# Two-layer cached attention and token mixer on one core: the last query tile of seven weights as two 64-row tiles, loaded in slices of 8 rows

## The chip, the core and the metric

The kernel runs on one core of a Trainium2 chip. A core has a matrix engine (TensorE, PE in the profile, with its weight loads PEld), a vector engine (VectorE, DVE), a scalar engine (ScalarE, ACT), GpSimd (POOL) and SyncE (SP), which here does nothing but issue transfers. Sixteen DMA engines move data between HBM and the on-chip memory (SBUF, 128 partitions). The metric is the device time of one execution in microseconds (us).

## The reference

Four blocks in a row on a state of 2 x 1 x 512 numbers: attention over a cache, mixer, attention, mixer. Both attention blocks read the same caches and the same weights.

```python
def _A_ref(x, k_cache, v_cache, wq, wo):          # B=2, D=512, 32 query heads, 8 KV heads
    q = (x @ wq).reshape(B, Sq, Hq, Dh)            # Dh=128, four query heads per KV head
    scores = q . k_cache * Dh ** -0.5              # 32768 cached keys per head
    o = softmax(scores) . v_cache
    return o.reshape(B, Sq, Hq * Dh) @ wo

def _B_ref(x, w1, b1, w2, b2):                     # mixer over a token axis of length 1, F=1792
    u = gelu(einsum("bsd,sf->bdf", layernorm(x), w1) + b1)
    return (einsum("bdf,fs->bds", u, w2) + b2).transpose

x = x + _A_ref(layernorm(x), ...)
x = x + _B_ref(layernorm(x), ...)
x = x + _A_ref(layernorm(x), ...)
x = x + _B_ref(layernorm(x), ...)
```

All numbers are float32. K and V together are 537 MB and are read in both layers; with the weights 1,067 MB go over the DMA engines (a few chunks stay on chip from one layer to the next).

## The kernel before

**Units and chunks.** A unit is one (layer, batch, KV head): 32 of them, in the order of the list `units`. The heads are split into `passing` (0, 1, 2, 3, 4, 6), whose units come first in layer 0 and last in layer 1, and `RESIDENT` (5, 7), whose units stand around the change of layer. A unit has 8 chunks of K and 8 of V, of 4,096 keys each; a chunk is 2 MB, 16 KB in each partition. `k_chunk` makes 8 products with a chunk of K, `v_chunk` 8 with one of V (16 rows each in the profile).

**Memory.** One tile `mem` holds 13 cells of 16 KB per partition and a rest of 5 x 2 KB. Cells 0 to 8 are the ring for K and V; cells 9 to 12 (`WCELL0`, `WCELLS`) hold the weights of up to four heads. In the middle of the run some cells and the rest keep a part of the K and V of head 7 (`KEPT_K`, `KEPT`).

**Weights.** For each head `wqo` has a row of 16 KB per partition: four tiles of wq (128 rows of the 512 inputs each, 512 columns) and four of wo. `load_weights` brings them in one transfer of 128 rows to one cell. `make_q` multiplies the normalised state `xnT` (128 partitions, 4 columns per batch) with the four wq tiles, each product a partial sum over 128 inputs; for passing heads both batches at once, the second one's query is kept (`q_kept`). `out_2` and `last_mixer` use the wo tiles through `wo_at`.

**The state.** `first_input` normalises the given state, which lies in 4 columns per batch. `to_columns` turns the row made by the mixer into such columns and normalises them into `xnT`.

**Order.** The kernel writes its own schedule. `stream` is the list of K and V loads in order; before the change of layer and after it a load is 4 chunks (8 MB) into one of two places of the ring, around the change it is one or two chunks. All work besides the chunks is entered by `at(time, f, ...)`, where time counts chunks; after each chunk `run(time)` emits what is due. A load of weights is entered 10 chunks before its unit's first K chunk (`kbeg[n] - 10`), the query's products 6 to 4 chunks before.

**SyncE's queue.** SyncE issues the loads in the order in which the program emits them. A K or V load waits until TensorE has finished with the chunks that lay in its place. Landings of loads are counted on eight semaphores in turn, so an issue also waits until the load eight issues earlier has landed. ScalarE issues three small transfers of its own: the state, the mixer's weights (`cols`) and one row of the output.

Of the kernel before, what the change touches and what calls it, by code (L numbers as in the profile page):

```python
# [13 lines left out]
P = 128  # L14
# [21 lines left out]
DIRECT = 2  # L36
TAIL_GROUPS = (3, 3, 3, 2, 1)
IDLE = (4, 1, 3, 2)
EPS = 1e-5


@with_exitstack
def gqa_mixer_kernel(ctx: ExitStack, tc: tile.TileContext, x, kt, v, wqo, cols, out):
# [38 lines left out]


    NP = 28 + 32 * 2
    widths = dict(x=B * DT, xn=B * DT, q=KEPT_Q * R, cols=4 * FT + 1, ident=P, one=1, half=1, selg=R * QT)
# [18 lines left out]
    def cells(k, m=1):  # L104
        return mem[:, k * CK : (k + m) * CK]

    def wq_at(h):
        return cells(home[h])[:, :W].rearrange("p (t c) -> p t c", t=DT)

    def wo_at(h):  # L110
        return cells(home[h])[:, W:].rearrange("p (t c) -> p t c", t=R)

    def load_weights(h, cell):
        home[h] = cell
        nc.sync.dma_start(cells(cell), wqo[h])


    used = [0] * (WCELL0 + WCELLS + 1)
# [80 lines left out]
    def first_input():  # L199

        t = spot()
        cen, sq = (t[:, k * B * DT : (k + 1) * B * DT].rearrange("p (b d) -> p b d", b=B) for k in range(2))
        m, rs = (t[:, (2 * DT + k) * B : (2 * DT + k + 1) * B] for k in range(2))
        p = misc()
        nc.tensor.matmul(p[:, : B * DT], ones, xcols.rearrange("p b d -> p (b d)"), start=True, stop=True)
        nc.vector.tensor_reduce(m, p[:, : B * DT].rearrange("p (b d) -> p b d", b=B), axis=AX.X, op=ALU.add)
# [4 lines left out]
        p = misc()  # L211
        nc.tensor.matmul(p[:, : B * DT], ones, sq.rearrange("p b d -> p (b d)"), start=True, stop=True)
        nc.vector.tensor_reduce(rs, p[:, : B * DT].rearrange("p (b d) -> p b d", b=B), axis=AX.X, op=ALU.add)
        nc.vector.tensor_scalar(rs, rs, 1.0 / D, EPS, op0=ALU.mult, op1=ALU.add)
        nc.gpsimd.tensor_tensor(rs, rs, half_neg.to_broadcast([P, B]), op=ALU.pow)
        for b in range(B):
            xT[b] = xcols[:, b, :]
            nc.vector.tensor_scalar_mul(xnT[:, :, b], cen[:, b, :], rs[:, b : b + 1])  # L218

    *ends, keeper = RESIDENT  # L220
# [30 lines left out]
    def to_columns(key):  # L251

        layer, b = key
        pt = misc()
        for d in range(DT):
            nc.tensor.matmul(  # L256
                pt[:, d : d + 1], ysb[key][:, d * P : (d + 1) * P], ident[:, :1], start=True, stop=True
            )
        nc.vector.tensor_scalar_add(xT[b], pt[:, :DT], b2c)
        mv, rs = stats[key]  # L260
        nc.vector.tensor_scalar(  # L261
            xnT[:, :, b], pt[:, :DT], mv[:, 0:1], rs, op0=ALU.subtract, op1=ALU.mult
        )

    def unit_of(n):

# [10 lines left out]
    def make_q(n, step, place=None):  # L277


        layer, b, h = unit_of(n)  # L280
        both = partner(n)
        m = 1 if both is None else B
        if n in q_kept:
            if step == 2:
                nc.vector.tensor_copy(qpad[n % 2][:, 28 : 28 + R], q_kept.pop(n))
            return
        if step == 0:

            q_ps[n] = pfix.tile([P, 512], F32, name="bcast") if N1 < n <= N3 + 2 else kept[0]
        if step < 2:  # L290
            for d in range(step * DT // 2, (step + 1) * DT // 2):
                nc.tensor.matmul(  # L292
                    q_ps[n][:m, :],
                    xnT[:, d, b : b + m],
                    wq_at(h)[:, d, :],
                    start=(d == 0),
                    stop=(d == DT - 1),
                )
# [234 lines left out]
    def out_2(n):  # L533
        layer, b, h = unit_of(n)
        for r in range(R):
            add_row(r, b, oT[n][:, r, :], wo_at(h)[:, r, :])

    ysb, px = {}, {}
    slope, shift, stats = {}, {}, {}
# [81 lines left out]
    def last_mixer(n):  # L621
# [9 lines left out]
        for k, to in enumerate((kept[1], acc)):  # L631
            for r in range(R):
                nc.tensor.matmul(
                    to[32 * r : 32 * r + 1, :w],
                    oT[n][:, r, 1:],
                    wo_at(h)[:, r, k * w : (k + 1) * w],
                    start=True,
                    stop=True,
                    skip_group_check=True,
                )  # L640
# [81 lines left out]
    def mix_4(key):  # L722

        layer, b = key
        p = px[key]
        nc.tensor.matmul(p, sel[b], ysb[key], start=False, stop=True, skip_group_check=True)
        if layer == LAYERS - 1:
            y = mem[:1, (WCELL0 + WCELLS) * CK :][:, :D]
# [166 lines left out]
def _layout(A_x, A_k_cache, A_v_cache, A_wq, A_wo, B_w1, B_b1, B_w2, B_b2):  # L895

    import numpy as np

    B, HKV, SK, DH = A_k_cache.shape
    D = A_x.shape[-1]  # L900
    n = SK // CK


    keys = np.arange(SK).reshape(n, CK)
    for c0, m in GROUPS:
        keys[c0 : c0 + m] = keys[c0 : c0 + m].reshape(P, m, CK // P).transpose(1, 0, 2).reshape(m, CK)
# [11 lines left out]
    return {  # L918
        "x": np.ascontiguousarray(A_x.reshape(B * (D // P), P).T),
        "kt": kt,  # L920
        "v": A_v_cache.reshape(B * HKV, SK * DH),
        "wqo": np.concatenate([wq.reshape(HKV, P, -1), wo.reshape(HKV, DH, -1)], axis=2),
        "cols": np.concatenate(cols, axis=1),
    }

# [24 lines left out]
```

## Time and profile before

| | |
|---|---|
| median of 3 runs | 2501.68 us (2501.5 to 2501.75) |
| the profiled execution | 2501.79 us |
| its span, first to last instruction | 2500.0 us |
| bytes moved by DMA | 1067.23 MB, mean 427 GB/s |
| TensorE busy | 1383.1 us (55%) |
| TensorE clock granted, mean | 0.773 |
| loads of weights | 14, of 2,048 KB, 33.8 us from issue to landing (median) |

How to read the profile. Its first part has the busy time of each engine and its share of the span. The second cuts the span into 40 slices; a digit is the busy share in tenths. The third has the DMA queues: q1 holds the transfers that SyncE issues, q10 those of ScalarE, q8 and q14 fetch instructions; the columns are packets, MB, and the time that the packets took as a share of 16 engines over the span. The DMA view can be cut to a stretch of the run: its packet counts and shares are then those of the packets that start in the stretch, and a share is of 16 engines over the stretch's length. A packet of 4 B is the mark by which one engine reports that its part of a transfer has landed. The fourth part follows back the chain of work that ended last. The rest are groups of instructions: line, engine, operation, names of output and inputs, shape, count, then busy time in us, mean duration in ns of one, and idle time of the engine before them. A float32 product appears as two rows of half the work. The timeline has start and duration in us. The windows view has, for each stretch, its length, the busy time and instructions of each engine (PE, PEld, DVE, ACT, POOL), the clock granted to TensorE, the mean busy share of the DMA engines and GB/s. The view of waits has, for an engine and a line, what it waited for, total us, times and the longest.

### The profile page before, as it was taken

The page shows a single profiled execution, that of the slowest core. Times are in us where ns is not written, and L with a number is a line of the kernel's source. Part 1 is how long each engine was busy: PE and PEld are TensorE (multiplying, and loading weights), DVE is VectorE, ACT ScalarE, POOL GpSimd, SP SyncE. Part 2 cuts the span into 40 slices and gives each one's busy share as a digit, 9 for nine tenths or more (in the row PEclk, how much of TensorE's full clock was granted, in tenths as well). Part 3 has the DMA queues.
Part 4 walks back from the last instruction along what each step waited for, and adds up shares of the span by engine and source line. Part 5 has one row for each costly group of instructions (what it writes and reads, how often), then busy time and mean ns, then how long its engine had stood idle before and what let it go on. Part 6 is the DMA issues. An engine that isn't in the chain of part 4 may idle for free.

```text
span 2500.0 us, 20528 instructions
## 1 busy us (share of the span) xinstructions
PE 1383.1 (55%) x9326; PEld 375.5 (15%) x9326; DVE 222.4 (9%) x610; ACT 185.4 (7%) x550; POOL 4.9 (0%) x17
## 2 busy tenths in 40 slices
PE   4545554645445554657667775455546454455546
PEld 1111111111111111111111211111111111111112
DVE  0000000000000000001111110000000000010002
ACT  0000000000000000001012010000000000011002
POOL 0000000000000000000000000000000000000000
PEclk8777777877777777879888977677778777777778
DMA  9999999999999999999999999999999999999996
GB/s 419 436 433 430 433 435 430 436 430 430 433 433 431 434 429 435 425 423 421 426 427 427 423 430 430 432 435 434 432 430 435 435 423 435 433 433 426 432 429 292
DMA packets 31200, 1067.23 MB, mean 427 GB/s; under 512 B 3717, under 2 KB 3721, under 8 KB 4618
## 3 DMA queue, kind: packets, MB, share of 16 engines
q1 hardware_dynamic: 30824, 1065.89, 99.2%
q8 instruction: 73, 1.20, 0.2%
q14 instruction: 13, 0.11, 0.0%
q10 hardware_dynamic: 290, 0.04, 0.0%
HBM read 1065.91 MB, written 0.00 MB: 426 GB/s over the span
## 4 chain that ended last, share of the span: by engine, by line
DMA 74%; PE 24%; issue 0%; DVE 0%; ACT 0%; SPq 0%; POOL 0%; ACTq 0%
DMA mem<-in_v_dram 65%; PE acc L492 19%; DMA mem<-in_kt_dram 9%; PE scores L359 3%; PE bcast L292 1%; PE rows L190 0%; PE small L385 0%; PE small L521 0%; ACT S L714 0%; PE kept L671 0%; PE small L379 0%; PE small L256 0%; ACT mem L681 0%; ACT mem L693 0%; PE bcast L575 0%
## 5 line engine op out<-in xcount | busy, mean ns | idle before, releaser
L359 PE MATMUL scores<-mem,small_sb 128*32 128x512 f32 x4096 | 620.6, 722 | 592.0 <-DMA mem<-in_kt_dram 591.6
L492 PE MATMUL acc<-mem,S 128*16 128x512 f32 x4088 | 614.1, 738 | 468.2 <-DMA mem<-in_v_dram 462.5
L359 PEld LDWEIGHTS scores<-mem,small_sb 128*32 128x32 f32 x4096 | 151.1, 127 | 970.5 <-issue 895.5
L396 ACT ACTIVATE S<-S,small_sb 128x128 f32<-128x128 f32 x240 | 123.5, 519 | 2102.4 <-DVE small_sb L387 1636.6
L492 PEld LDWEIGHTS acc<-mem,S 128*16 128x16 f32 x4088 | 134.8, 110 | 831.7 <-issue 693.2
L369 DVE TENSOR_REDUCE small_sb<-scores 128x1 f32<-128x512 f32 x64 | 44.2, 691 | 874.1 <-PE scores L359 874.1
L391 DVE STREAM_TRANSPOSE S<-scores 128x512 f32<-128x512 f32 x64 | 45.4, 710 | 131.4 <-PE acc L492 131.4
L292 PE MATMUL kept<-mem,small_sb 128*2 128x512 f32 x104 | 50.9, 615 | 1.7 <-DVE small_sb L218 1.7
L190 PE MATMUL rows<-mem,small_sb 128*1 128x512 f32 (+1 forms) x276 | 48.4, 603 | 3.1 <-ACT mem L714 2.4
L396 ACT ACTIVATION_READ_ACCUMULATOR S<-S,small_sb 128x1 f32 x240 | 44.8, 187 | 0.0
L381 DVE TENSOR_REDUCE small_sb<-small 1x4 f32<-1x128 f32 x32 | 8.8, 276 | 280.7 <-PE small L379 280.7
L460 DVE SCALAR_TENSOR_TENSOR S<-acc,small_sb,S 128x128 f32<-128x128 f32 x93 | 32.6, 351 | 3.3
L523 DVE RECIPROCAL small_sb<-small 128x4 f32<-128x4 f32 x32 | 5.9, 185 | 292.1 <-PE small L521 292.1
L531 DVE TENSOR_TENSOR small_sb<-small,small_sb 128x4 f32<-128x4 f32 x31 | 5.1, 164 | 278.2 <-PE small L529 278.2
L714 ACT ACTIVATE S<-bcast,small_sb 128x512 f32<-128x512 f32 x28 | 20.7, 775 | 96.1 <-DVE small_sb L583 82.6
L190 PE MATMUL rows<-S,small_sb 128*1 128x512 f32 (+1 forms) x56 | 21.2, 591 | 8.1 <-ACT S L714 8.1
L304 PE MATMUL small<-small_sb,mem 2*128 2x2 f32 x112 | 15.1, 252 | 17.9 <-DVE mem L301 17.9
L458 DVE TENSOR_SCALAR S<-acc,small_sb 128x128 f32<-128x128 f32 x31 | 10.8, 350 | 128.8 <-PE acc L492 128.8
L292 PE MATMUL bcast<-mem,small_sb 128*1 128x512 f32 (+1 forms) x40 | 19.1, 609 | 1.2 <-DVE small_sb L261 1.2
L529 PEld LDWEIGHTS small<-small_sb,S 128*128 128x128 f32 x62 | 11.6, 234 | 48.8 <-issue 36.0
L304 PEld LDWEIGHTS small<-small_sb,mem 2*128 2x128 f32 x112 | 13.9, 190 | 30.5 <-DVE mem L301 27.3
L529 PE MATMUL small<-small_sb,S 128*128 128x4 f32 x62 | 14.3, 301 | 4.9 <-DVE S L460 4.9
(132 smaller groups left out, 267.7 us busy)
## 6 DMA issues: line engine op xcount, KB each, us to landing
mem<-in_kt_dram SPq DMA_DIRECT2D x44, 2048.0 KB, 12.7
mem<-in_v_dram SPq DMA_DIRECT2D x35, 2048.0 KB, 13.9
mem<-in_v_dram SPq DMA_DIRECT2D x9, 4096.0 KB, 32.7
mem<-in_wqo_dram SPq DMA_DIRECT2D x14, 2048.0 KB, 33.8
mem<-in_kt_dram SPq DMA_DIRECT2D x7, 4096.0 KB, 25.7
mem<-in_v_dram SPq DMA_DIRECT2D x2, 1280.0 KB, 13.6
mem<-in_v_dram SPq DMA_DIRECT2D x2, 768.0 KB, 18.6
mem<-in_v_dram SPq DMA_DIRECT2D x4, 256.0 KB, 28.8
```

The source lines that it names most:

```text
L190: nc.tensor.matmul(rows[32 * g : 32 * g + b + 1, :], weights if b else weights[:, 1:], row, start=False, stop=True, skip_group_check=True,)
L292: nc.tensor.matmul(q_ps[n][:m, :], xnT[:, d, b : b + m], wq_at(h)[:, d, :], start=(d == 0), stop=(d == DT - 1),)
L304: nc.tensor.matmul(pt[:, r * m : (r + 1) * m], q_row[n][:m, r * DH : (r + 1) * DH], ident[:m, :m], start=True, stop=True,)
L359: nc.tensor.matmul(sc_ps[n, half][32 * g : 32 * g + 32, :], q, kc[:, (k * NG + g) * w : (k * NG + g + 1) * w], start=(i == 0 and k == 0), ...
L369: nc.vector.tensor_reduce(mx[n][:, half : half + 1], sc_ps[n, half], axis=AX.X, op=ALU.max)
L391: nc.vector.transpose(S[half], sc_ps[n, half])
L396: nc.scalar.activation(s[:, :, h], s[:, :, h], AF.Exp, bias=neg[n][:, h : h + 1], scale=SCALE, accum_out=lsum[n][:, half, h : h + 1],)
L458: nc.vector.tensor_scalar_mul(t, acc[:, :DH], mask[:, 0:1])
L460: nc.vector.scalar_tensor_tensor(t, acc[:, k * DH : (k + 1) * DH], mask[:, k : k + 1], t, op0=ALU.mult, op1=ALU.add)
L492: nc.tensor.matmul(acc[32 * g : 32 * g + R * QT, :], S[half][:, col : col + R * QT], (own if q < stay else vc)[:, q * w : (q + 1) * w], st ...
L529: nc.tensor.matmul(po[:, :R], asb, selh, start=True, stop=True)
L714: nc.scalar.activation(hid[key, f], px[key], AF.Gelu_apprx_tanh, bias=shift[key][:, f : f + 1], scale=slope[key][:, f : f + 1],)
```

## The change

The layout in HBM puts the four wo tiles ahead of the last wq tile, so that this tile stands at the end of each row of 16 KB. `x` gets a fifth column per batch: the fourth one with its two halves swapped, so that inputs 448 to 511 also stand in partitions 0 to 63; `xnT` gets the same fifth column, in `first_input` and in `to_columns` (one more product and one more VectorE operation on 64 partitions).

For seven weights (layer 0: heads 2, 3, 4, 6; layer 1: heads 2, 3, 4) `load_weights` loads only 14 KB of each row. The last wq tile goes as two tiles of 64 rows to partitions 0 to 63: one to the end of the weight's cell, one to the rest behind the cells. `load_slice` loads 8 of these rows, 2 KB each, every fourth partition; 16 slices make up the 128 rows. They are entered one by one, every second chunk in layer 0 (from 42 to 12 chunks before the unit), two in three chunks in layer 1. `make_q` then has five products instead of four, the last two over 64 rows. The row that the mixer of batch 0 writes in layer 1 moves to another place of the rest.

```diff
+HALF = 64
...
-    widths = dict(x=B * DT, xn=B * DT, ...)
+    widths = dict(x=B * (DT + 1), xn=B * (DT + 1), ...)
...
+    def part(h, k):
+        return cells(home[h])[:, k * D : (k + 1) * D]
+
+    def rest(k):
+        return mem[:, (WCELL0 + WCELLS) * CK :][:, k * D : (k + 1) * D]
+
     def wq_at(h):
-        return cells(home[h])[:, :W].rearrange("p (t c) -> p t c", t=DT)
+        parts = [(P, k, part(h, k)) for k in range(DT - 1)]
+        if not uneven[h]:
+            return parts + [(P, DT - 1, part(h, DT - 1 + R))]
+        return parts + [(HALF, DT - 1, part(h, DT - 1 + R)), (HALF, DT, rest(home[h] - WCELL0))]
...
+    def load_weights(h, cell, split=False):
+        home[h], uneven[h] = cell, split
+        if split:
+            n = (DT - 1 + R) * D
+            nc.sync.dma_start(cells(cell)[:, :n], wqo[h][:, :n])
+        else:
+            nc.sync.dma_start(cells(cell), wqo[h])
+
+    def load_slice(h, cell, j):
+        n = (DT - 1 + R) * D
+        k, j = divmod(j, HALF // 8)
+        p = j // 4 * 32 + j % 4
+        to = rest(cell - WCELL0) if k else cells(cell)[:, n:]
+        nc.sync.dma_start(to[p : p + 29 : 4], wqo[h][k * HALF + p : k * HALF + p + 29 : 4, n:])
...
+        nc.tensor.matmul(pt[:HALF, DT : DT + 1], ysb[key][:, D - HALF :], ident[:, :1], start=True, stop=True)
         nc.vector.tensor_scalar_add(xT[b], pt[:, :DT], b2c)
         mv, rs = stats[key]
-        nc.vector.tensor_scalar(
-            xnT[:, :, b], pt[:, :DT], mv[:, 0:1], rs, op0=ALU.subtract, op1=ALU.mult
-        )
+        for p, c, n in ((P, 0, DT), (HALF, DT, 1)):
+            nc.vector.tensor_scalar(
+                xnT[:p, c : c + n, b], pt[:p, c : c + n], mv[:p, 0:1], rs[:p], op0=ALU.subtract, op1=ALU.mult
+            )
...
-            for d in range(step * DT // 2, (step + 1) * DT // 2):
+            parts = wq_at(h)
+            for p, d, w in parts[2:] if step else parts[:2]:
                 nc.tensor.matmul(
...
+                    q_ps[n][:m, :], xnT[:p, d, b : b + m], w[:p], start=(d == 0), stop=(d == len(parts) - 1)
                 )
...
+    def slice_times(n, h):
+        m = 2 * HALF // 8
+        if units[n][0] == 0:
+            return [kbeg[n] - 42 + 2 * j for j in range(m)] if h in passing[2:] else []
+        k = passing[-KEPT_Q:-1].index(h) if h in passing[-KEPT_Q:-1] else None
+        return [] if k is None else [kbeg[N3 + 2] + (2, 26, 58)[k] + 3 * j // 2 for j in range(m)]
...
-            at(kbeg[n] - 10, load_weights, h, (again if layer else weight_cell)[h])
+            slices = slice_times(n, h)
+            cell = (again if layer else weight_cell)[h]
+            at(kbeg[n] - 10, load_weights, h, cell, len(slices) > 0)
+            for j, time in enumerate(slices):
+                assert time < kbeg[n] - 6
+                at(time, load_slice, h, cell, j)
...
+    x = A_x.reshape(B, D // P, P).transpose(2, 0, 1)
+    x = np.concatenate([x, np.roll(x[:, :, -1:], HALF, axis=0)], axis=2)
...
-        "wqo": np.concatenate([wq.reshape(HKV, P, -1), wo.reshape(HKV, DH, -1)], axis=2),
+        "wqo": np.concatenate([a.reshape(HKV, P, -1) for a in (wq[:, :, :-1], wo, wq[:, :, -1])], axis=2),
```

More of the change, by code (lines that the diff above doesn't have):

```diff
@@ L84, in gqa_mixer_kernel @@
     NP = 28 + 32 * 2
-    widths = dict(x=B * DT, xn=B * DT, q=KEPT_Q * R, cols=4 * FT + 1, ident=P, one=1, half=1, selg=R * QT)
+    widths = dict(x=B * (DT + 1), xn=B * (DT + 1), q=KEPT_Q * R, cols=4 * FT + 1, ident=P, one=1, half=1, selg=R * QT)
     widths |= dict(selh=R, mask=QT, others=B, oz=2 * R * B, qpads=NP, unit=2 * 16, ln=16 + 2 * FT)
@@ L105, in cells, with wo_at @@
         return mem[:, k * CK : (k + m) * CK]
+    def part(h, k):
+        return cells(home[h])[:, k * D : (k + 1) * D]
+    def rest(k):
+        return mem[:, (WCELL0 + WCELLS) * CK :][:, k * D : (k + 1) * D]
     def wq_at(h):
-        return cells(home[h])[:, :W].rearrange("p (t c) -> p t c", t=DT)
[L110 to L115, printed above, removed]
+        parts = [(P, k, part(h, k)) for k in range(DT - 1)]
+        if not uneven[h]:
+            return parts + [(P, DT - 1, part(h, DT - 1 + R))]
+        return parts + [(HALF, DT - 1, part(h, DT - 1 + R)), (HALF, DT, rest(home[h] - WCELL0))]
+    def wo_at(h, r):
+        return part(h, DT - 1 + r)
+    uneven = {}
+    def load_weights(h, cell, split=False):
[11 more added lines that the diff above has]
+        nc.sync.dma_start(to[p : p + 29 : 4], wqo[h][k * HALF + p : k * HALF + p + 29 : 4, n:])
     used = [0] * (WCELL0 + WCELLS + 1)
@@ L201, in first_input, with total @@
         t = spot()
[L202 to L206, printed above, removed]
+        n = B * (DT + 1)
+        cen, sq = (t[:, k * n : (k + 1) * n].rearrange("p (b d) -> p b d", b=B) for k in range(2))
+        m, rs = (t[:, 2 * n + k * B : 2 * n + (k + 1) * B] for k in range(2))
+        def total(dst, src):
+            p = misc()[:, :n]
+            nc.tensor.matmul(p, ones, src.rearrange("p b d -> p (b d)"), start=True, stop=True)
+            by = p.rearrange("p (b d) -> p b d", b=B)[:, :, :DT]
+            nc.vector.tensor_reduce(dst, by, axis=AX.X, op=ALU.add)
+        total(m, xcols)
         nc.vector.tensor_scalar_mul(m, m, 1.0 / D)
@@ L210, in first_input @@
         nc.vector.tensor_mul(sq, cen, cen)
-        p = misc()
-        nc.tensor.matmul(p[:, : B * DT], ones, sq.rearrange("p b d -> p (b d)"), start=True, stop=True)
-        nc.vector.tensor_reduce(rs, p[:, : B * DT].rearrange("p (b d) -> p b d", b=B), axis=AX.X, op=ALU.add)
+        total(rs, sq)
         nc.vector.tensor_scalar(rs, rs, 1.0 / D, EPS, op0=ALU.mult, op1=ALU.add)
@@ L216, in first_input @@
         for b in range(B):
-            xT[b] = xcols[:, b, :]
+            xT[b] = xcols[:, b, :DT]
             nc.vector.tensor_scalar_mul(xnT[:, :, b], cen[:, b, :], rs[:, b : b + 1])
@@ L290, in make_q @@
         if step < 2:
-            for d in range(step * DT // 2, (step + 1) * DT // 2):
+            parts = wq_at(h)
+            for p, d, w in parts[2:] if step else parts[:2]:
                 nc.tensor.matmul(
[L293 to L297, printed above, removed]
+                    q_ps[n][:m, :], xnT[:p, d, b : b + m], w[:p], start=(d == 0), stop=(d == len(parts) - 1)
                 )
@@ L535, in out_2 @@
         for r in range(R):
-            add_row(r, b, oT[n][:, r, :], wo_at(h)[:, r, :])
+            add_row(r, b, oT[n][:, r, :], wo_at(h, r))
     ysb, px = {}, {}
@@ L635, in last_mixer @@
                     oT[n][:, r, 1:],
-                    wo_at(h)[:, r, k * w : (k + 1) * w],
+                    wo_at(h, r)[:, k * w : (k + 1) * w],
                     start=True,
@@ L727, in mix_4 @@
         if layer == LAYERS - 1:
-            y = mem[:1, (WCELL0 + WCELLS) * CK :][:, :D]
+            y = rest(WCELLS)[:1]
             nc.vector.tensor_scalar_add(y, p[:1, :], b2c[:1, :])
@@ L918, in _layout @@
     return {
-        "x": np.ascontiguousarray(A_x.reshape(B * (D // P), P).T),
+        "x": x.reshape(P, -1),
         "kt": kt,
         "v": A_v_cache.reshape(B * HKV, SK * DH),
-        "wqo": np.concatenate([wq.reshape(HKV, P, -1), wo.reshape(HKV, DH, -1)], axis=2),
+        "wqo": np.concatenate([a.reshape(HKV, P, -1) for a in (wq[:, :, :-1], wo, wq[:, :, -1])], axis=2),
         "cols": np.concatenate(cols, axis=1),
```

## The prediction

> **What bounds the kernel now.** I read the page first: its engine shares, the DMA line of its slices, the queues and the chain of waits.
>
> ```profile
> span 2500.0 us, 20528 instructions
> PE 1383.1 (55%) x9326; PEld 375.5 (15%) x9326; DVE 222.4 (9%) x610; ACT 185.4 (7%) x550; POOL 4.9 (0%) x17
> ...
> DMA  9999999999999999999999999999999999999996
> ...
> q1 hardware_dynamic: 30824, 1065.89, 99.2%
> q8 instruction: 73, 1.20, 0.2%
> ...
> DMA 74%; PE 24%; issue 0%; DVE 0%; ACT 0%; SPq 0%; POOL 0%; ACTq 0%
> ```
>
> No compute engine is near full; the 16 DMA engines carry packets of SyncE's queue for 99.2% of the span. A change that only moves bytes can matter through nothing but these 16. The windows view prices a byte:
>
> ```profile
> 300.00:700.00 400.00, 203.91 (x1384) 55.36 (x1388) 27.63 (x79) 21.43 (x80) 0.00 (x0) 0.74 1.00 432
> ```
>
> 432 GB/s over 16 engines is 27.0 GB/s each, so a row of 2,048 B inside a long row costs one engine 0.076 us.
>
> Next, whether the engines run dry between loads. The timeline of SyncE and PE:
>
> ```profile
> 605.41 0.33 SPq L344 DMA_DIRECT2D mem<-in_kt_dram  x1
> ...
> 617.12 3.63 PE L492 MATMUL acc<-mem,S 128*16 128x512 f32 x32
> ...
> 620.81 0.33 SPq L446 DMA_DIRECT2D mem<-in_v_dram  x1
> 631.11 1.94 PE L359 MATMUL scores<-mem,small_sb 128*32 128x512 f32 x8 [10.36 <-DMA mem<-in_kt_dram]
> ```
>
> SyncE issues the V load when PE has emptied its buffer (617.12 + 3.63 = 620.75), and the K load before it lands only at 631.1. A queue thus has about 10 us of work left when the next load is added.
>
> Last, whether the 16 are alike. Each load ends with one 4 B landing packet per engine, so the DMA view cut to short stretches counts engines that have finished one load. Four stretches: 46 to 47, 646.3 to 647.5, 647.5 to 649.3, 649.3 to 651.4.
>
> ```profile
> DMA packets 32, 1.05 MB, mean 1049 GB/s; under 512 B 16, under 2 KB 16, under 8 KB 16
> ```
> ```profile
> DMA packets 24, 1.05 MB, mean 874 GB/s; under 512 B 8, under 2 KB 8, under 8 KB 8
> ...
> DMA packets 5, 0.33 MB, mean 182 GB/s; under 512 B 0, under 2 KB 0, under 8 KB 0
> ...
> DMA packets 23, 0.98 MB, mean 468 GB/s; under 512 B 8, under 2 KB 8, under 8 KB 8
> ```
>
> At 46 us all 16 finish within 1 us. At 647 us eight have finished a load, nothing lands for 1.8 us, and the other eight follow: an **early half** and a **late half**, 3 to 3.5 us apart by the middles of their stretches (646.9 and 650.35). PE needs all 16, so the late half sets the pace and the early half's lead is spare. What makes half of them late? The queue of instruction fetches is the only other steady load; its rows for one fetch (597 to 600) and for 0 to 650, 650 to 1150, 1150 to 2490:
>
> ```profile
> q8 instruction: 1, 0.02, 2.2%
> ...
> q8 instruction: 17, 0.28, 0.2%
> ...
> q8 instruction: 14, 0.23, 0.2%
> ...
> q8 instruction: 41, 0.67, 0.2%
> ```
>
> One fetch occupies an engine for 2.2% x 16 x 3 us = 1.06 us. On eight engines, 17 fetches make 2.3 us each; the trace shows 3 to 3.5, less some 0.3 from the start, so I count 1.3 us of delay per fetch (bounds 1.06 and 1.5). All 72 give each late engine 9 x 1.3 = 11.7 us more work than an early one has (9.5 to 13.5).
>
> **The change, part by part.** *Bytes moved.* In seven weights (heads 2, 3, 4, 6 of layer 0 and 2, 3, 4 of layer 1) the load loses 2,048 B of each of its 128 rows, eight rows an engine: 16,384 B, 0.61 us less on every engine. The 16 slices of such a weight bring these rows back on eight engines, one row each per slice. The price of a 2 KB row by itself comes from the last pieces of V (2481.62 to 2482.03), that of a landing packet from the one-row store (2331.39 to 2331.40):
>
> ```profile
> DMA packets 41, 0.07 MB, mean 175 GB/s; under 512 B 6, under 2 KB 6, under 8 KB 41
> ...
> q1 hardware_dynamic: 41, 0.07, 46.4%
> ```
> ```profile
> q10 hardware_dynamic: 1, 0.00, 5.6%
> ```
>
> 46.4% x 16 x 0.41 = 3.04 us for 35 rows and 6 landings; a landing is 5.6% x 16 x 10 ns = 9 ns, so a row is 85 ns and a slice 94 ns on its engine. Sixteen: 1.50 us. Net per weight: 1.50 - 0.61 = +0.89 us on the eight that carry slices, -0.61 us on the others; over seven weights **+6.2 and -4.25 us**. Bounds of a slice: 76 ns (bytes alone) below; above, the 430 ns that one issue takes SyncE (row below), which no engine shows; I take 94, its own kind of packet.
>
> *Which eight.* Rows go p, p+4, ... p+28 in partitions 0 to 63. The only load or store of few rows in mid-run, the one-row store from partition 0, sends its packet in 2328.90 to 2328.95 and its landing at 2331.39. Five rows of 64 KB later (65,536 B / 27.0 = 2.42 us each, so 2343.48) one load's landing falls in 2343.46 to 2343.49, among the first eight (2343.2 to 2344.9):
>
> ```profile
> q10 hardware_dynamic: 1, 0.00, 10.5%
> ```
> ```profile
> DMA packets 2, 0.07 MB, mean 2185 GB/s; under 512 B 1, under 2 KB 1, under 8 KB 1
> ...
> DMA packets 20, 0.79 MB, mean 463 GB/s; under 512 B 8, under 2 KB 8, under 8 KB 8
> ```
>
> So the engine that serves partition 0's store is an early one; I take slices to run on the early half. The Trainium skill, page "DMA: Bandwidth & Descriptors", section "The descriptor swizzle", gives partitions 0 to 63 to engines 0 to 7, and its section on the semaphore's 16 puts a load of 8 rows on the lowest eight; the store's packet agrees. The same page's "Rules for kernel authors" speaks against such a change: transfers to one half of the partitions spray over all 16 engines. For 64 rows at once that would shift nothing; 8 rows cannot be split over 16.
>
> *The sum by stretch.* Slices of layer 0 run from about 60 to 690 us. By then the late half has 4 x 0.61 = 2.4 us less work, the early half 4 x 0.89 = 3.6 us more, against a lead of 3 to 3.5: the halves are level or the early one is last, and nothing is won yet. Fetches go on: by 1150 the late half is 31/8 x 1.3 = 5.0 us behind before, now 2.6, the early half 3.6: won 1.4. From 1150, 41 fetches make 6.7, now 4.9 (three weights, -1.8), against 2.7 on the early half: won 1.8. If the queues empty around 1150 and start level, the gains add to 3.2; if they never do, the totals count: 11.7 against max(11.7 - 4.25, 6.2) = 7.45, won 4.25. I take 3.7.
>
> *SyncE.* 112 issues more, at most as long as a weight's:
>
> ```profile
> L115 SPq DMA_DIRECT2D mem<-in_wqo_dram x14: 393/427/438, 0.7 to 1982.8; - x14
> ...
> SPq L344 <- DMA mem<-in_kt_dram: 591.8, 68, 25.9
> SPq L344 <- PE scores L359: 549.0, 65, 13.2
> SPq L446 <- PE acc L492: 495.9, 61, 11.6
> SPq L446 <- DMA mem<-in_v_dram: 424.6, 60, 13.6
> ```
>
> 112 x 0.43 = 48 us, at two or three between loads about 1 us each time, inside the more than 2,000 us that SyncE waits and the 10 us of margin: nothing. Without that cover it would be 48. Behind a waiting slice stand the next K or V load and then PE; but each slice goes to columns whose last reader is a product many chunks back, so I count no wait.
>
> *PE and VectorE.* An uneven weight's query takes one more product:
>
> ```profile
> L292 PE MATMUL kept<-mem,small_sb 128*2 128x512 f32 x104 | 50.9, 615 | 1.7 <-DVE small_sb L218 1.7
> L256 PE MATMUL small<-small_sb,S 128*128 128x1 f32 x16 | 2.1, 253 | 0.0
> L261 DVE TENSOR_SCALAR small_sb<-small,small_sb 128x4 f32<-128x4 f32 x2 | 0.5, 272 | 0.0
> ```
>
> Thirteen queries of four products make 104 rows, two passes each: 1.23 us, seven times 8.6 us of a PE that is 55% busy. Its data landed earlier: PE reaches the query after chunks whose loads stand behind the slices. The return to columns gains two passes and one VectorE step, 2 x 0.25 + 0.27 = 0.8 us, twice, on the short chain between layers. The DMA view's share there is full:
>
> ```profile
> 1180.00:1200.00 20.00, 14.98 (x90) 4.60 (x86) 6.43 (x13) 0.63 (x1) 0.54 (x1) 0.87 1.01 429
> ```
>
> Hidden, then; uncovered it is 1.6. The first normalisation on 10 columns for 8 comes before any K chunk has landed: nothing.
>
> **Sum.** The profiled execution took 2501.79 us, 1.8 around its span of 2500.0; the three runs' median is 2501.68. Span 2500.0 - 3.7 = 2496.3, with 1.7 around it: **2498.0**.
>
> **Rivals.**
> *The early half overtakes (2500.9).* With 1.06 us a fetch the lead at 690 us is only 2.6; the early half then ends 1.0 us later than the late one did before. If the queues level out there, that loss stays, 650 to 1150 wins nothing and the last stretch 1.8: won 0.8. For it: 2.2% for a fetch. Against: the measured lead of 3 or more.
>
> *A slice costs its engine more than its packet (2507.0).* Place: the early half's queues. It decides from 112x - 4.25 = 11.7, x = 142 ns; at twice the row, 190 ns, the early half has 17.0 us more and ends 5.3 after the old late half. For it: no row shows loads of one row per engine back to back. Against: the 85 and 9 ns. The Trainium skill's page "SBUF — State Buffer", section "The DMA setup-cost knee", has about 2 us fixed per transfer: 112 in series would be 224 us; here transfers queue behind one another, and the rows of the last V pieces follow each other without such a pause.
>
> *The slices run on the late half (2507.9).* Then +6.2 falls on the engines that set the end. Against: the store's packet.
>
> *SyncE stands at a slice until it has landed (about 2560).* Its rows show waits for landings. Then the next load is issued only when the one before has left the queue. What an empty queue costs is seen at the start, in the stretches 0 to 1.75 and 0 to 1.85 after the first issue:
>
> ```profile
> 0.74 0.39 SPq L115 DMA_DIRECT2D mem<-in_wqo_dram  x1
> ```
> ```profile
> DMA packets 0, 0.00 MB, mean 0 GB/s; under 512 B 0, under 2 KB 0, under 8 KB 0
> ...
> DMA packets 2, 0.03 MB, mean 18 GB/s; under 512 B 0, under 2 KB 0, under 8 KB 0
> ```
>
> 1.1 us dry, by an estimate in each of 56 pairs of slices, is 62 us on the forecast. Against: no two slices share bytes.
>
> *More than the sum (2495.5).* A level pair of halves also shortens the stalls at the layers' ends (416 GB/s against 432 in this row, 1.5 us):
>
> ```profile
> 1140.00:1180.00 40.00, 29.87 (x184) 8.28 (x180) 8.84 (x22) 12.26 (x16) 0.54 (x1) 0.91 0.99 416
> ```
>
> **How the numbers follow.** Forecast 0.64 (own range 2496.6 to 2499.2, from the two sums 4.25 and 3.2 with a fetch at its bounds); early half overtakes 0.12; dearer slice 0.10; late half 0.06; more than the sum 0.05; SyncE stands 0.03. The range 2496.2 to 2504 holds the forecast, the overtaking and the cheaper half of the dearer slices, about 0.8. 0.2% is 5.0 us, about what a measurement of this kernel can tell from no change. Faster than 2496.7: more than the sum and the forecast's edge, 0.10. Slower than 2506.7: late half, half of the dearer slices, SyncE, 0.14. Same: 0.76.
>
> **What would show it.** Landings of one load after 690 us: the two halves within 3 us of each other, in the other order around 700, nearly level at 1100 and at the end. Time at the 690 us mark unchanged within 1 us, the gain after it. Slices' packets of 2 KB at 85 ns. SyncE's waits for PE unchanged. Landings at 2343 still 8 and 8 more than 3 us apart would mean the wrong engines; SyncE waiting for the weights' landings between chunk loads, the blocked queue; slices above 140 ns, the dearer one.

## The result and the profile after

The changed kernel took **2509.73 us** (median of 7 runs, 2509.24 to 2510.65), the kernel before, beside it, 2501.79 (7 runs, 2501.5 to 2502.65). The ratio is 1.0032, 95% interval 1.0020 to 1.0044. The forecast was 2498.0 with a range up to 2504: the time lies above the range, on the other side of no change. The profiled execution took 2509.60, 1.8 of it around its span.

The page of the changed kernel, the lines that answer to those of before:

```profile
span 2507.8 us, 20687 instructions
PE 1390.9 (55%) x9344; PEld 374.7 (15%) x9344; DVE 222.8 (9%) x612; ACT 185.5 (7%) x550; POOL 4.9 (0%) x17
...
DMA  9999999999999999999999999999999999999996
...
q1 hardware_dynamic: 32616, 1065.90, 99.0%
q8 instruction: 73, 1.20, 0.2%
...
DMA 75%; PE 24%; DVE 0%; issue 0%; ACT 0%; SPq 0%
...
mem<-in_wqo_dram SPq DMA_DIRECT2D x112, 16.0 KB
```

The picture is that of before: the same bytes, the same fetches, the DMA engines full, no compute engine nearer to its limit. Only the packets are more, 1,792 of them: 112 slices of 8 rows and 8 landings. So each slice runs on eight engines, as forecast. With the totals unchanged, I look for the 8 us in how the work is spread over the engines.

SyncE's waits in the changed kernel (engine, line, what it waited for; total us, times, longest), and the durations of its issues (ns: least, median, most):

```profile
SPq L377 <- PE scores L392: 554.5, 67, 14.6
SPq L377 <- DMA mem<-in_kt_dram: 533.3, 66, 25.8
SPq L479 <- PE acc L525: 492.8, 61, 11.4
...
SPq L145 <- DMA mem<-in_kt_dram: 20.5, 4, 11.1
...
SPq L145 <- DMA mem<-in_v_dram: 9.5, 2, 5.2
```
```profile
L145 SPq DMA_DIRECT2D mem<-in_wqo_dram x112: 623/640/984, 58.2 to 1863.0; - x112
```

L377 issues the loads of K, L479 those of V. SyncE waits for TensorE as before (554.5 and 492.8 us against 549.0 and 495.9). At a slice (L145) it waits six times in 112, 30 us in all. A slice's issue takes 640 ns, not 430, but SyncE's waits cover it.

Now the landings. The DMA view counts one 4 B packet for each engine that has finished a load. First a load of the kernel before at 2244 to 2249 us, in three stretches (2243.9 to 2245.0, to 2247.7, to 2248.6), then the same load of the changed kernel (2251.4 to 2253.9, to 2255.6, to 2256.8); no slices run there any more.

```profile
DMA packets 16, 0.52 MB, mean 477 GB/s; under 512 B 8, under 2 KB 8, under 8 KB 8
...
DMA packets 17, 1.06 MB, mean 391 GB/s; under 512 B 0, under 2 KB 0, under 8 KB 0
...
DMA packets 16, 0.52 MB, mean 583 GB/s; under 512 B 8, under 2 KB 8, under 8 KB 8
```
```profile
DMA packets 30, 1.05 MB, mean 419 GB/s; under 512 B 14, under 2 KB 14, under 8 KB 14
...
DMA packets 10, 0.60 MB, mean 352 GB/s; under 512 B 0, under 2 KB 0, under 8 KB 0
...
DMA packets 13, 0.72 MB, mean 601 GB/s; under 512 B 2, under 2 KB 2, under 8 KB 2
```

Before, eight engines were early and eight late. After, fourteen have landed, then nothing for 1.7 us, then **two engines alone**. TensorE waits for all 16, so these two set the end. The reading to test: of the eight engines that carry slices, six were early ones and could afford it; two were late ones.

Which two? The trace doesn't name a packet's engine, but an engine starts a packet where it ended the one before (3 or 4 ns ahead of its end), so a fetch can be followed to the next landing. Two fetches of the changed kernel, each with the landing that follows (stretches 316.75 to 316.78 and 330.40 to 330.43; 456.84 to 456.87 and 470.36 to 470.38):

```profile
q8 instruction: 1, 0.02, 213.8%
...
DMA packets 2, 0.00 MB, mean 68 GB/s; under 512 B 1, under 2 KB 1, under 8 KB 2
...
q8 instruction: 1, 0.02, 201.2%
...
DMA packets 2, 0.07 MB, mean 3277 GB/s; under 512 B 1, under 2 KB 1, under 8 KB 1
```

The first fetch takes 213.8% x 16 x 30 ns = 1.03 us, to 317.79. Five rows of 2.42 us later, and 0.5 us more, comes a landing, and behind it a row of 2 KB: this engine takes fetches **and** slices. The second, 0.97 us, leads in the same way to 470.37, and behind that landing stands the next row of 64 KB: fetches, no slice. So a fetch delays its engine by about 1.5 us, its own 1.0 and 0.5 on the packet behind it. Fetches go round eight engines: the row of 64 KB behind a fetch takes between 2.89 and 2.97 us, and the same values come back with every eighth fetch. Of the fetches between 200 and 700 us that can be followed without doubt, the ones in two neighbouring places of the round led to slices (at 277, 317 and 600 us, and at 559 us one load further on). These are the two places with a row of 2.97 us. The fetches in the other six places led to no slice.

### The profile page after: what moved, and what is told of

It is laid out like the page before. It is cut to its first block, busy times and chain, and to the rows that moved or that the text cites. A ratio compares the mean times of both kernels' runs of the same rounds, so it can differ in the third digit from the quotient of the medians.

```text
span 2507.8 us, 20687 instructions
## 1 busy us (share of the span) xinstructions
PE 1390.9 (55%) x9344; PEld 374.7 (15%) x9344; DVE 222.8 (9%) x612; ACT 185.5 (7%) x550; POOL 4.9 (0%) x17
## 4 chain that ended last, share of the span: by engine, by line
DMA 75%; PE 24%; DVE 0%; issue 0%; ACT 0%; SPq 0%
DMA mem<-in_v_dram 64%; PE acc L525 19%; DMA mem<-in_kt_dram 11%; PE scores L392 3%; PE bcast L329 0%; PE small L418 0%; PE rows L220 0%; PE small L554 0%; PE small L412 0%; PE kept L704 0%; ACT S L747 0%; ACT mem L714 0%; PE bcast L759 0%; ACT mem L726 0%; DVE S L441 0%
## 5 line engine op out<-in xcount | busy, mean ns | idle before, releaser
L329 PE MATMUL kept<-mem,small_sb 128*2 128x512 f32 (+1 forms) x118 | 56.8, 605 | 1.7 <-DVE small_sb L252 1.7
L337 PE MATMUL small<-small_sb,mem 2*128 2x2 f32 x112 | 14.7, 249 | 17.8 <-DVE mem L334 17.8
L412 PE MATMUL small<-small_sb 128*1 128x128 f32 x64 | 17.7, 373 | 0.8 <-DVE small_sb L408 0.8
L337 PEld LDWEIGHTS small<-small_sb,mem 2*128 2x128 f32 x112 | 13.5, 186 | 30.4 <-DVE mem L334 27.2
```

Of the source, the lines that this page charges most:

```text
L329: nc.tensor.matmul(q_ps[n][:m, :], xnT[:p, d, b : b + m], w[:p], start=(d == 0), stop=(d == len(parts) - 1))
L337: nc.tensor.matmul(pt[:, r * m : (r + 1) * m], q_row[n][:m, r * DH : (r + 1) * DH], ident[:m, :m], start=True, stop=True,)
L412: nc.tensor.matmul(pm[:1, :P], mxa, ident, start=True, stop=True)
```

## The experiments

The kernel before ran beside each group: 2501.74 (runs 1 to 3), 2501.91 (4 to 7), 2502.06 (8 to 10), 2501.75 (11 and 12). Each number is a median of four to ten runs.

**1. Without slices.**

```diff
-                at(time, load_slice, h, cell, j)
+                pass
...
-        return parts + [(HALF, DT - 1, part(h, DT - 1 + R)), (HALF, DT, rest(home[h] - WCELL0))]
+        return parts
```

> The seven weights keep their rows of 14 KB, and the 112 slices are left out: the last query tile of these weights is neither loaded nor multiplied, so the result lacks 128 of the 512 inputs of their queries. Theory A (two of the eight engines that carry the slices are among the late ones, which also take the instruction fetches; these two set the end): without slices every engine has 7 x 0.61 = 4.3 us less, so 2501.8 - 4.3 = 2497.5, from 2496.5 to 2499. Theory B (the 112 more transfers cost time whichever engines carry them: by the order of the queue, by SyncE's issues or by dry spells): the same 2497.5. Theory C (fewer bytes are worth nothing, since dry spells give them back): 2501 to 2502.5.

Measured: 2500.04 (2498.99 to 2501.48), ratio 0.9992 (0.9983 to 1.0002), between the ranges of theories A and B and that of C. The bytes are worth some 1.7 us of the 4.3, and the slices then cost 9.7 of the changed kernel's time. 112 rows of 84 ns, each with 2 ns or so around it, make 9.6 us on one engine: the cost has the size of the slices' whole time on an engine that sets the end.

**2 and 3. Other slices of the same rows.** Run 2, with `STRIPES` as (first, end, step) of a slice's partitions:

```diff
+STRIPES = [(j, j + 61, 4) for j in range(4)]
...
-        k, j = divmod(j, HALF // 8)
-        p = j // 4 * 32 + j % 4
+        k, j = divmod(j, len(STRIPES))
+        p, e, s = STRIPES[j]
...
-        nc.sync.dma_start(to[p : p + 29 : 4], wqo[h][k * HALF + p : k * HALF + p + 29 : 4, n:])
+        nc.sync.dma_start(to[p:e:s], wqo[h][k * HALF + p : k * HALF + e : s, n:])
...
```

> The same two tiles of 64 rows, but in slices of 16 rows (every fourth partition): 8 transfers a weight for 16, 56 for 112, and every one of the 16 engines carries one row of each. Per weight and engine 8 x 86 ns less 614 ns = +0.07 us, +0.5 us over seven weights. Theory A: 2502.3, from 2501.3 to 2503.5, though the fifth product, the fifth column and the split are all still there. Theory B: half as many transfers, half of the 8 us: 2505.8; if it goes by rows, 2509.7.

Run 3:

```diff
+STRIPES = [(j, j + 51, 10) for j in range(10)] + [(60, 64, 1)]
```

> Slices of 6 rows (every tenth partition) and of 4 for what is left: 22 transfers a weight for 16, 154 for 112. If a load of k rows goes to the k lowest engines, engines 6 and 7 carry none; engines 0 to 3 get 22 x 86 ns less 614 = +1.28 us a weight (+9.0 over seven), 4 and 5 +1.1 us (+7.7), the other ten -4.3. Theory A with engines 6 and 7 as the two that also take fetches: the late ones end 4.3 us earlier and the six early ones have 9.0 of a lead that the fetches (9 x 1.55 us) make 14 in all but only 3.5 by 690 us: 2498 to 2503. Theory A with other two: +9 on a late engine, 2509 to 2512. Theory B: more transfers, 2509.7 to 2513.

Measured: 2512.29 (ratio 1.0043, 1.0028 to 1.0058) and 2522.31 (1.0082, 1.0066 to 1.0099). Both were meant to relieve the late engines and both are slower than the changed kernel. Neither theory had these times. Around the slices, rows of 64 KB took up to 0.2 us (run 2) and 0.3 us (run 3) longer than their 2.42 us, on engines that carried no slice at that moment too. The sums of the durations of these rows are 7.4 and 11.4 us an engine above run 1. Run 3 has two faults more: SyncE waited 156 us at its slices, and its six engines include a late one, as runs 4 and 9 will show. These edits changed two things at once, the engines and the partitions each engine writes, and so the next runs change one.

**4, 5, 6 and 9. The same slices, cut to the first 6, 7, 4 and 5 of their 8 rows**, with the product of the last tile left out as in run 1. K stands for the number of rows.

```diff
-        nc.sync.dma_start(to[p : p + 29 : 4], wqo[h][k * HALF + p : k * HALF + p + 29 : 4, n:])
+        nc.sync.dma_start(to[p : p + 4 * K - 3 : 4], wqo[h][k * HALF + p : k * HALF + p + 4 * K - 3 : 4, n:])
```

> Slices of the changed kernel cut to their first 6 rows of 8 (partitions p to p + 20, every fourth); the other rows of the last query tile aren't loaded, and the seven weights leave its product out, so the result lacks 128 inputs of their queries. With no slices at all such a kernel took 2500.0, with 8 rows 2509.7: 9.7 us, which is what 112 rows of 86 ns cost one engine (9.6). Theory A (of the eight engines two are late ones, the last two in order): the six that are left are early and the time is that without slices, 2500.0 to 2501.5. Theory A with the two elsewhere among the eight, or theory D (no engine has a lead that is worth anything, each row on any engine is paid): 2509 to 2510.

> The same with 7 rows of 8 (p to p + 24). Theory A with the last two of the eight engines late: the seventh still sets the end, 2508.5 to 2510. If only the eighth is late: 2500 to 2501.5. Theory D: 2509 to 2510.

> The same with 4 rows of 8 (p to p + 12). Theory A with the late two behind the first four: 2500.0 to 2501.5, as with six. Late ones among the first four, or theory D: 2509 to 2510.

> 5 rows of 8 (p to p + 16), product left out. Of the first six engines one is late (six rows cost 9.7 us, four none). If it is the fifth: 2509 to 2510; if the sixth: 2499 to 2501.5. Nothing between.

| rows of a slice | us | ratio, 95% interval |
|---|---|---|
| none | 2500.04 | 0.9992 (0.9983 to 1.0002) |
| 4 | 2499.45 | 0.9990 (0.9981 to 1.0000) |
| 5 | 2499.49 | 0.9989 (0.9980 to 0.9999) |
| 6 | 2509.43 | 1.0028 (1.0018 to 1.0038) |
| 7 | 2509.38 | 1.0030 (1.0020 to 1.0040) |
| 8 (the change) | 2509.73 | 1.0032 (1.0020 to 1.0044) |

There is a step of 10 us at the sixth row and nothing else. Four or five engines carry 112 rows each for nothing; the sixth pays them in full. Theory D (each row on any engine is paid) falls, and so does the guess that the late ones are the last two in order. The landings of one load each say how many late engines carry slices: the run with 6 rows (2055.6 to 2058.0, to 2060.7, to 2060.9), then the run with 7 (2251.3 to 2253.6, to 2255.1, to 2256.1).

```profile
DMA packets 31, 1.05 MB, mean 437 GB/s; under 512 B 15, under 2 KB 15, under 8 KB 15
...
DMA packets 14, 0.92 MB, mean 340 GB/s; under 512 B 0, under 2 KB 0, under 8 KB 0
...
DMA packets 2, 0.07 MB, mean 326 GB/s; under 512 B 1, under 2 KB 1, under 8 KB 1
```
```profile
DMA packets 30, 1.05 MB, mean 456 GB/s; under 512 B 14, under 2 KB 14, under 8 KB 14
...
DMA packets 5, 0.33 MB, mean 218 GB/s; under 512 B 0, under 2 KB 0, under 8 KB 0
...
DMA packets 13, 0.72 MB, mean 721 GB/s; under 512 B 2, under 2 KB 2, under 8 KB 2
```

One engine stands alone with 6 rows, two with 7, and still two with 8. So **the sixth and the seventh of the eight are late ones**, the first five and the eighth early. The product that is left out here and done in the changed kernel costs too little to be seen: the last two rows of the table are 0.35 us apart, inside the noise.

The Trainium skill, page "DMA: Bandwidth & Descriptors", section "Why a DMA increments its semaphore by 16 and not by 1", has as many engines as the largest divisor up to 16 of the rows. The time from 5 to 6 rows and the landings from 6 to 7 agree: each row more brought in one engine more.

**7 and 8. The same engines, other partitions.** Run 7 is the whole change with its two tiles in partitions 64 to 127. Run 8 is the run with 4 rows, but the last four of the eight.

```diff
-        nc.sync.dma_start(to[p : p + 29 : 4], wqo[h][k * HALF + p : k * HALF + p + 29 : 4, n:])
+        nc.sync.dma_start(to[HALF + p : HALF + p + 29 : 4], wqo[h][(1 - k) * HALF + p : (1 - k) * HALF + p + 29 : 4, n:])
...
```

> The whole change, but the two tiles of 64 rows go to partitions 64 to 127 (the fifth column of the state holds the other half there). Where a load's rows are given to engines by their order, the same eight engines carry the slices, but into partitions that other engines write in the large loads. Theory P (two engines that write the same partitions' port slow each other; the 16-row and 6-row slices showed packets of 65,536 B stretched by 100 to 210 ns around them, 7.5 and 11 us in all): 2509.7 plus a stretch of that kind, 2513 to 2522. Without such a port: 2509.7. If the engines go by partition, the slices run on the other eight without stretch, six of which are then late: 2509 to 2511, with six engines last in place of two.

```diff
-        nc.sync.dma_start(to[p : p + 29 : 4], wqo[h][k * HALF + p : k * HALF + p + 29 : 4, n:])
+        nc.sync.dma_start(to[p + 16 : p + 29 : 4], wqo[h][k * HALF + p + 16 : k * HALF + p + 29 : 4, n:])
```

> As the run with 4 rows (2499.45), but the other four of the 8 rows: partitions p + 16 to p + 28 for p to p + 12; the product of the last tile is left out as there. Were engines given by order, the same four early engines carry these rows, into partitions that the next four engines write in the large loads. Theory P (a slice into partitions that another engine is writing slows both): half as many rows as the slices to partitions 64 to 127 (16.8 us for 896 rows), so 2499.5 + 4 to 9 = 2503.5 to 2508.5, with packets of 65,536 B longer than 2.42 us about the slices. Without P: 2499 to 2501. If the engines go by partition, two late ones carry slices: 2509.

Measured: 2526.47 (1.0097, 1.0080 to 1.0114), 16.7 us more than the changed kernel with the same rows of HBM and the same count; and 2513.93 (1.0047, 1.0032 to 1.0062), 14.5 us more than the first four rows. Both are above their ranges (2522 and 2508.5). SyncE's waits at the slices, 33 and 30 us, are those of the change, so they don't explain it. The DMA view of 130 to 640 us, first for the run with the first four rows, then for the one with the last four (packets and MB; q1 as before):

```profile
DMA packets 4518, 220.21 MB, mean 432 GB/s; under 512 B 651, under 2 KB 651, under 8 KB 851
...
q1 hardware_dynamic: 4501, 219.96, 99.9%
```
```profile
DMA packets 4482, 217.45 MB, mean 426 GB/s; under 512 B 656, under 2 KB 656, under 8 KB 858
...
q1 hardware_dynamic: 4466, 217.21, 99.8%
```

The engines are just as full and move 2.76 MB less in 510 us, 6.4 us of their time. It isn't idle time but longer packets: a row of 2 KB still takes 84 ns; the rows of 64 KB in flight around it, on all 16 engines, take up to some 0.3 us more. Over the whole run these rows take 11.1 us an engine more in run 8 than in run 6, and 14.2 more in run 7 than in the change; the rest of the 14.5 and 16.7 us stays open. (The traced execution of run 6 took 2502.05 us, the longest of its ten.)

Did the slices stay on the same engines? The fetches tell, since the two late engines of the eight are those whose row behind a fetch takes 2.97 us. In run 7 such a fetch (461.90 to 461.93) leads to a landing with a row of 2 KB behind it (478.265 to 478.28); so do the other three of that kind that can be followed in layer 0, and none of another place of the round does. In run 8 one (605.64 to 605.67) leads to a landing with the next row of 64 KB behind it (616.87 to 616.88), and so does the other late engine's, at 279 us:

```profile
q8 instruction: 1, 0.02, 211.7%
...
DMA packets 2, 0.00 MB, mean 137 GB/s; under 512 B 1, under 2 KB 1, under 8 KB 2
```
```profile
q8 instruction: 1, 0.02, 212.1%
...
DMA packets 2, 0.07 MB, mean 6554 GB/s; under 512 B 1, under 2 KB 1, under 8 KB 1
```

So the engine goes by the row's place in the load and not by its partition: by partition run 8's slices would have run on these two, and run 7's would have left them. Theory P stands as far as this: where a slice goes matters, apart from who carries it, and the slices of the change, row k to partitions p + 4k, are laid out so that this costs nearly nothing (the 64 KB rows of run 6 sum to 0.2 us an engine more than those of run 1). That the cause is a port into the memory which the engine shares with the one that writes these partitions in the large loads is argued, not shown. The Trainium skill's page "SBUF — State Buffer", section "Door 1: The DMA port swizzle (why `[64,N]` ≈ `[32,N]`)", has 16 such ports, each with four neighbouring partitions and the four that lie 32 above them, and by its table the rows of run 8 go to the ports of the fifth to the eighth engine, those of run 7 to ports of the other eight; both times agree with it.

**10 and 11. How much lead the early engines have.** Run 10 issues each of the 4-row slices twice; run 11 issues them once, with rows of 4 KB. Nothing reads what comes in addition; the product is left out.

```diff
-        k, j = divmod(j, HALF // 8)
+        i, j = divmod(j, HALF // 8)
+        k = i % 2
...
-        to = rest(cell - WCELL0) if k else cells(cell)[:, n:]
-        nc.sync.dma_start(to[p : p + 29 : 4], wqo[h][k * HALF + p : k * HALF + p + 29 : 4, n:])
+        to = rest((cell - WCELL0 + i) % 5) if i else cells(cell)[:, n:]
+        nc.sync.dma_start(to[p : p + 13 : 4], wqo[h][k * HALF + p : k * HALF + p + 13 : 4, n:])
...
-        m = 2 * HALF // 8
+        m = 4 * HALF // 8
...
```

> 4 rows, but 32 slices a weight for 16 (each row twice, the second time to a place that nothing reads; product left out): engines 0 to 3 get 224 x 86 ns less 4.3 = +15.0 us, the others -4.3. It measures the lead of the early engines. If all the delay that fetches give the late ones (9 x 1.55 = 14 us) is spare, as the prediction had it for the whole run: 2499.5 to 2503. If only the lead of the moment is spare (3 to 5 us between the landings of one load): 15.0 - 4 = 11 over before, about 2513. By stretch, with 3.5 us spare at 690 us and layer 0 adding 8.6: 2506 to 2508.

```diff
-        to = rest(cell - WCELL0) if k else cells(cell)[:, n:]
-        nc.sync.dma_start(to[p : p + 29 : 4], wqo[h][k * HALF + p : k * HALF + p + 29 : 4, n:])
+        to = mem[:, (WCELL0 + WCELLS) * CK :][:, 2 * k * D : (2 * k + 2) * D]
+        nc.sync.dma_start(to[p : p + 13 : 4], wqo[h][k * HALF + p : k * HALF + p + 13 : 4, n - D :])
```

> The run with 4 rows again, with the same 112 transfers, but rows of 4,096 B for 2,048 (the extra bytes and the rest go where nothing reads; product of the last tile left out). It measures the lead of the early engines without the waits of SyncE for landings that 224 transfers brought. A row of 4,096 B is some 162 ns: engines 0 to 3 get 112 x 162 ns less 4.3 = +13.9 us, layer 0 +7.9 of them, the others -4.3. If the whole 14 us of fetch delay is spare: 2499.5 to 2502.5. If only the lead of the moment is: layer 0 gives 7.9 - 3.5 = 4.4 late, and layer 1 6.0 less 0 to 4: 2508 to 2512.5. If SyncE's waits were what made the run with 224 transfers slow: 2499.5 to 2502.5 too, and then its trace has to have the early engines first to land.

Measured: 2514.30 (1.0049, 1.0034 to 1.0064) and 2510.55 (1.0033, 1.0021 to 1.0046). Run 10 can't be read alone: SyncE now stood at slices (L146) until earlier loads had landed, 424 us over 53 times.

```profile
SPq L146 <- DMA mem<-in_kt_dram: 223.5, 23, 13.5
SPq L146 <- DMA mem<-in_v_dram: 179.9, 24, 9.5
SPq L146 <- DMA mem<-in_wqo_dram: 20.7, 6, 4.3
```

Run 11 waits 32 us at its slices, the change 30. Its landings of a load after the slices of layer 0 (750.8 to 753.2, to 756.7, to 758.3):

```profile
DMA packets 28, 1.05 MB, mean 437 GB/s; under 512 B 12, under 2 KB 12, under 8 KB 12
...
DMA packets 24, 1.57 MB, mean 449 GB/s; under 512 B 0, under 2 KB 0, under 8 KB 0
...
DMA packets 15, 0.72 MB, mean 451 GB/s; under 512 B 4, under 2 KB 4, under 8 KB 4
```

The four that carry the slices are now the last, behind the twelve others by 3.5 us of silence. The last of them lands at 758.1 us; in the kernel before the same load ended at 753.1, 5.0 earlier, where the expectation by the lead of the moment had 4.4. The time lies in the range of that expectation (2508 to 2512.5). So **only the lead of the moment is spare**, 3 to 5 us. In the kernel before, the first and the last landing of one load are less than 6 us apart wherever loads can be told apart, though the whole run's delay is more than twice that. With 5.4 us of net load on four engines (run 6) the lead isn't used up; with 13.9 it is, though the fetches' delays add up to about 13.5 us.

**12. 64 rows at once.**

```diff
+STRIPES = [(0, 64, 1)]
```

> The whole change, its two tiles of 64 rows loaded by one transfer each (partitions 0 to 63), 14 transfers for 112. The prediction said that 64 rows at once shift nothing. If 16 engines carry 4 rows of each and nothing else matters: 8 x 85 ns less 614 = +0.07 us a weight, 2500 to 2502.5. Theory P: half of the 16 engines write into partitions that the others write in the large loads. By the 16-row slices (12.3 us over the run without slices, of which 4.8 are rows) 7.5 more, so 2507 to 2512; should two engines share what one has alone, 4 rows take the time of 8: 14 x 0.34 us = 4.8, 2505 to 2508. If 64 rows go to eight engines only: 2509 to 2511.

Measured: 2517.79 (1.0064, 1.0049 to 1.0079), above all that was expected. Fourteen transfers in place of 112 are 8 us slower than the change. Rows of 64 KB behind these loads took 0.2 to 0.9 us more in the trace. The Trainium skill's section "Door 1", named above, has half of the ports for partitions 0 to 63; that the time is longer agrees, and its size wasn't foreseen.

No version that beats both kernels was tried. Runs 6 and 9 leave work out and still win only 2.5 us on the kernel before. By an estimate from these runs, to carry all 128 rows of seven weights, five engines would get 7 x (25.6 x 0.086 - 0.61) = 11 us each, most of the way to run 11, which lost 8.8.

## Why the prediction was wrong

*What bounds the kernel*: right. The time moved with the work of the last of the 16 engines; in runs 2, 3, 7, 8 and 12 that work also grew by longer rows, which the prediction didn't have.

*The price of a fetch*: 1.3 us counted, about 1.5 measured, near its upper bound. Nine of them make the late engines' delay 13.5 us, not 11.7, and that doesn't explain the miss.

*The price of a slice*: right. 94 ns counted; 84 and a landing of 9 in the trace, 86 ns by the steps between packets, since they overlap a little. The rival of the dearer slice falls.

*Which eight: this is the step that failed.* The prediction showed one engine early, the one that serves a store from partition 0, and wrote "I take slices to run on the early half". One engine was extended to eight. The fetches' eight and the slices' eight aren't each other's complement: they share two, the sixth and the seventh. The two halves in the landings say how many are late, not which. The Trainium skill's rule that a load of 8 rows goes to the lowest eight (the section on the semaphore's 16, named above) is contradicted by no run, but no trace here shows an engine's number; that the lowest eight are the early eight was the prediction's own step.

*The sum.* With two late engines under the slices the gain on the others is worth nothing, and the price is that of the rival "the slices run on the late half", 2507.9, given 0.06. It came nearest, 1.8 us low. Its net of 6.2 took the saved bytes at 4.25; run 1 won 1.7. The slices are paid in full, 9.6, and 9.6 - 1.7 = 7.9 is the 7.9 that was measured; the agreement is closer than run 1, whose runs spread over 2.5 us, can warrant.

*The gain by stretch*: 3.7 counted, 1.7, 2.5 and 2.6 measured where slices cost nothing (runs 1, 6, 9). Too large, but of the right sign. Why fewer bytes win only this stays open. Had the eight all been early, the change would, by an estimate from runs 6 and 9, have taken about 2499.5: inside the range, 1.5 above the forecast.

*The early half overtakes*: not in the change. Run 11 shows the mechanism with more load, and its point of decision is the lead of the moment, as that rival had it, not the whole run's total.

*SyncE, TensorE, VectorE at nothing*: right. SyncE's waits also covered 640 ns an issue. With and without the added product the time is the same (2509.73 and 2509.38), and runs 6 and 9, which keep the added column, are faster than the kernel before. Run 10 shows the waits that come when slices stand twice as densely, not what they alone cost.

*"For 64 rows at once that would shift nothing"*: wrong, by run 12: 17.8 us over the run without slices.

*What would show it*: the sign named for the wrong engines was 8 and 8 still more than 3 us apart; what came was 14 and 2, a mixture that wasn't thought of.

## What to carry to other kernels

When every consumer waits for the last of 16 engines, a transfer of few rows has to be costed on the engine that is last, and each engine that it uses has to be shown early by itself; a sample of one isn't a half. Cut the transfer row by row: the step in the time names the engine. A lead is worth what it is when the work is added, not what it would sum to over the run.

## What was not expected of the hardware

A small transfer can slow engines that don't carry it. Its rows take their 84 ns in any case, but when the small rows go to partitions other than those of the change, rows of 64 KB take longer: those in flight up to 0.4 us (run 7), those behind a transfer of 64 rows 0.2 to 0.9. The costs: 14.5 us for 448 rows of 2 KB (run 8 against 6), 16.7 us for 896 (run 7), 17.8 for 14 transfers of 64 rows (run 12 against 1; 4.8 of it are the rows' own time, 56 an engine at 85 ns). Why is not shown.

The instruction fetches go round eight of the 16 engines, two of them among the eight that carry a load of 8 rows, and each delays its engine by about 1.5 us, half as much again as its own packet.
